# Value loads on a second DMA queue, and the last loads and products in another order: an adaLN attention and MLP block on one core

## The chip, the core and the metric

The kernel runs on one core of a Trainium2 chip. The core has engines that run side by side, each with its own instruction stream: TensorE (PE, matrix products, whose weight loads are listed as PEld), VectorE (DVE), ScalarE (ACT), GpSimd (POOL) and SyncE (SP, which only issues transfers). Transfers from main memory (HBM) to on-chip memory are carried by 16 DMA engines, which all queues share; a queue is where an engine puts the transfers it issues. The metric is the time on the device in microseconds, as the median over runs. A change of 0.2% is about the least that a measurement of this kernel can tell from none.

## The reference

Two tokens (B = 2, one position each, D = 512) go through one transformer block whose normalisations are shifted, scaled and gated by a condition `c`:

```
mod = (silu(c) @ w_mod).reshape(2, 6, 1, -1)            # sa, ca, ga, sb, cb, gb
h = layernorm(x) * (1 + ca) + sa
q = h @ wq                                              # 32 heads of 128
k, v = the last W = 4096 positions of k_cache, v_cache  # 8 key/value heads, each for 4 query heads
o = softmax(q k^T * 128**-0.5) v
x = x + ga * (o @ wo)
h = layernorm(x) * (1 + cb) + sb
x = x + gb * (silu(h @ w1) @ w2)                        # F = 1792
```

All is float32. There is little arithmetic for each byte: the weights and the two windows of the caches, 97.5 MB, are read once.

## The kernel before

**The ring.** All large loads go through one ring of eight slots (`slots`, 16 KB per partition each). `stream(n)` hands out the next n slots in turn, starting on a multiple of n where n is even. A load into a slot waits until all readers of what the slot held before are done. `load_pair(cache, s)` (L77) takes two slots for one step's keys or values (two key/value heads of one token, 4 MB), and `load_runs` (L88) takes as many as a stretch of rows of a weight needs. Both issue from SP, whose queue is worked off in order: a load whose slot is not free holds back all that stand behind it.

**The steps.** Attention runs in `STEPS` = 8 steps (L477). In step s, `keys(s, j)` (L356) has DVE transpose the keys in 32 x 32 blocks, in four parts; `scores(s, j)` (L366) multiplies each part with the queries on PE; `maxima` and `exponentials` (L382, L400) take the softmax on DVE and ACT; `turn(s)` (L415) brings the probabilities into the order that the value product needs (DVE, PE, then two ACT instructions that write `ptb`); `weighted(s)` (L445) is the value product on PE, 32 matmul instructions, which ends with an ACT copy to `ob`; `collect(s)` (L460) adds the result into `o_all`. The work is staggered: step s turns the probabilities of step s - 1 and forms their value product after its own scores. `place` (L312) lays out the queries; its first half runs before step 0, its second in step 2. The step before the last turns its own probabilities at its end.

**The loads around the steps.** `fetch(s)` (L349) issues the keys of step s and the values of step s - 1, so the order on SP is w_mod, x, wq, K0, K1, V0, K2, V1, K3, ... K7, V6, V7, and then wo in two loads (rows 0 to 23 of each partition's 32, then 24 to 31), w1 in two and w2 in four. In the ring this puts V7 into the slots of K6, the first wo load into those of V5 and the first of K7's, w1's first load into those of V6, the rest of w1 and the first w2 load into those of V7, and the later w2 loads into those of wo.

**The tail.** After the last step come the division by the row sums, the product with wo (`acc_o`, L579, and `ao`, L588), the residual and second normalisation, the product with w1 (`hid`, L627), silu, the product with w2 (`acc_yw`, L661, `acc_y`, `acc_l`) and the output. `busy(n)` (L562) puts n filler matmuls (two instructions each) on a scratch bank `junk` into PE's order at fixed places.

**Order.** A planner orders the instructions of each engine; an instruction marked with `inorder` (`tc.keep_in_program_order`) stays behind everything traced earlier on its engine. An unmarked one may move forward to where the planner takes its inputs as ready. The matmuls, transposes and copies of the steps are marked; the loads are not.

Of the kernel before, what the change touches and what calls it, by code (L numbers as in the profile page):

```python
# [23 lines left out]
def adaln_block(  # L24
# [19 lines left out]
    nc = tc.nc  # L44
# [19 lines left out]
    def bank(tag, name):  # L64
        return (psum1 if tag in "CO" else psum).tile([P, 512], F32, tag=tag, name=name)
# [4 lines left out]
    def stream(n=1):  # L70
        i = turn_of[0]
        if n % 2 == 0:
            i += -i % n
        turn_of[0] = i + n
        return slots[:, i % RING : i % RING + n, :].rearrange("p s e -> p (s e)")

    def load_pair(cache, s):  # L77


        i, b = divmod(s, B)  # L80
        t = stream(2)
        nc.sync.dma_start(
            t,
            cache[b, 2 * i : 2 * i + 2, SK - W :, :].rearrange("e (u n) d -> u e (n d)", u=P // 2),
        )
        return t

    def load_runs(w, per, lo, hi):  # L88

        e = w.shape[1]  # L90
        n = -(-(hi - lo) * e // 4096)
        t = stream(n)[:, : (hi - lo) * e].rearrange("p (q e) -> p q e", e=e)
        nc.sync.dma_start(t, w.rearrange("(p q) e -> p q e", q=per)[:, lo:hi, :])
        return t


# [2 lines left out]
    x_sp, c_sp = xc[:, 0, :], xc[:, 1, :]  # L99
    nc.vector.memset(xc, 0.0)  # L100
    wm = load_runs(w_mod, 4, 0, 4)
    rows8 = lambda t: t.rearrange("(ab r) m -> ab r m", r=16)[:, 0, :]
    for b in range(B):
        for lo in (0, 2):
# [3 lines left out]
            )  # L108
    nc.sync.dma_start(rows8(x_sp), x2.rearrange("b (g m) -> g b m", m=P))  # L109
    wqt = load_runs(wq, 4, 0, 4)  # L110


# [199 lines left out]
    def place(n):  # L312

        qT = once.tile([P, D], F32, tag="wide", name=f"qT{n}").rearrange("p (s j r) -> p s j r", s=4, r=32)
        inorder(nc.vector.transpose(qT.rearrange("p s j r -> p (s j r)"), q_ps[n]))  # L315
        for g in range(G):
            r = slice(32 * g, 32 * g + 32)
            eng = nc.gpsimd if g % 2 else nc.vector
            inorder(eng.tensor_copy(  # L319
                qg[n][r, :, :, :, g], qT[r, :, :, 0:32:16].rearrange("p s j b -> p s b j")  # L320
            ))
        rp = bank("C", f"qr{n}")[:, :P]
        inorder(nc.tensor.matmul(  # L323
            rp, rep4, qg[n].rearrange("p s b j g -> p (s b j g)"), start=True, stop=True
        ))
        for i in range(4):
            r = slice(32 * i, 32 * i + 32)
            cp = nc.scalar.copy if i % 2 else nc.vector.tensor_copy
            inorder(cp(
                qbd[n][r].rearrange("p s b j c -> p (s b j) c")[:, :, 4 * i : 4 * i + 4],  # L330
                rp[r, :].rearrange("p (m g) -> p m g", g=G),
            ))
# [12 lines left out]
    STEPS = B * HKV // 2  # L345
    kt, vt, wot, kT = {}, {}, [], {}
    s_ps, pr, o_ps, o_sb = {}, {}, {}, {}

    def fetch(s):  # L349

        if s < STEPS:
            kt[s] = load_pair(k_cache, s)
        if s > 0:
            vt[s - 1] = load_pair(v_cache, s - 1)

    def keys(s, j):  # L356


        kT[s, j] = ktp.tile([P, 64, 32], F32, tag="kT", name=f"kT{s}_{j}")
        for c in range(2):  # L360
            inorder(nc.vector.transpose(  # L361
                kT[s, j][:, 32 * c : 32 * c + 32, :],
                kt[s].rearrange("p (n j r) -> p j n r", j=4, r=32)[:, j, 32 * c : 32 * c + 32, :],
            ))

    def scores(s, j):  # L366

        if j == 0:
            s_ps[s] = bank("A", f"s{s}")
        i, b = divmod(s, B)  # L370
        for c in range(2):
            for e in range(2):
                r, h = 64 * e + 32 * c, 2 * i + e
                inorder(nc.tensor.matmul(  # L374
                    s_ps[s][r : r + 32, :],
                    qbd[h // 4][:, h % 4, b, j, :],
                    kT[s, j][:, 32 * c : 32 * c + 32, e:32:2],
                    start=(j == 0),
                    stop=(j == 3),
                ))  # L380

    def maxima(s):  # L382
        mx = work.tile([P, 1], F32, tag="mx", name=f"mx{s}")
        inorder(nc.vector.tensor_reduce(mx, s_ps[s], axis=AX.X, op=ALU.max))  # L384
        mT = bank("B", f"mT{s}")
        inorder(nc.tensor.matmul(mT[0:1, :P], mx, ident, start=True, stop=True))  # L386
        m = mrow[s % 2]
        mg = work.tile([1, 2, G], F32, tag="mg", name=f"mg{s}")
        inorder(nc.vector.tensor_reduce(
            mg,  # L390
            mT[0:1, :P].rearrange("o (e c i g) -> o e g c i", e=2, c=2, g=G)[:, :, :, :, 0:4],
            axis=AX.XY,
            op=ALU.max,
        ))
        inorder(nc.vector.tensor_copy(
            m.rearrange("o (e c i g) -> o e c i g", e=2, c=2, g=G)[:, :, :, 0:4, :],
            mg[:, :, None, None, :].to_broadcast([1, 2, 2, 4, G]),
        ))
# [16 lines left out]
    def turn(s):  # L415

        xp = once.tile([P, 16, 32], F32, tag="xp", name=f"xp{s}")
        inorder(nc.vector.transpose(xp, pr[s]))  # L418
        zp = once.tile([P, 4, 16, 16], F32, tag="zp", name=f"zp{s}")
        inorder(nc.vector.tensor_mul(  # L420
            zp,
            xp[:, None, :, 0:16].to_broadcast([P, 4, 16, 16]),
            quarter[:, :, None, None].to_broadcast([P, 4, 16, 16]),
        ))
        tp = bank("C", f"pT{s}")[:, : 2 * P]
        for i in range(4):
            inorder(nc.tensor.matmul(  # L427
                tp[32 * i : 32 * i + 32, :],
                mix.rearrange("p v e -> p (v e)"),
                zp.rearrange("p y t x -> p (y t) x")[:, :, 4 * i : 4 * i + 4],  # L430
                start=True,
                stop=True,
            ))
        for e in range(2):
            inorder(nc.scalar.activation(  # L435
                ptb[s % 2][:, :, e, :],
                tp.rearrange("p (w z) -> p w z", z=16),
                AF.Copy,
                scale=odd[:, e : e + 1],
            ))  # L440

    def weighted(s):


        o_ps[s] = bank("D", f"o{s}")  # L445
        for w in range(16):
            r = 32 * (w % 4)
            inorder(nc.tensor.matmul(  # L448
                o_ps[s][r : r + 32, :],
                ptb[s % 2][:, w].rearrange("p e z -> p (e z)"),  # L450
                vt[s].rearrange("p (c w m f d) -> p c f w m d", c=2, w=4, m=4, f=2)[
                    :, w // 8, w // 4 % 2, w % 4
                ],
                start=(w < 4),
                stop=(w >= 12),
            ))
        o_sb[s] = once.tile([P, 4 * DH], F32, tag="wide", name=f"ob{s}")
        inorder(nc.scalar.copy(o_sb[s], o_ps[s]))  # L458

    def collect(s):  # L460

        i, b = divmod(s, B)
        lo = 2 * HQ - 8 - (HQ * b + 2 * G * i)
        for m in range(4):
            r = 64 * (m % 2)
            inorder(nc.tensor.matmul(  # L466
                o_all[r : r + 64, :],
                selh[:, m, lo : lo + 2 * HQ],
                o_sb[s][:, m * DH : (m + 1) * DH],
                start=(s == 0 and m < 2),  # L470
                stop=(s == STEPS - 1 and m >= 2),
                skip_group_check=True,
            ))

    fetch(0)
    keys(0, 0)
    for s in range(STEPS + 1):  # L477
        if s < STEPS:
            fetch(s + 1)
            scores(s, 0)  # L480
        if s > 0 and s != STEPS - 1:
            turn(s - 1)
        if s > 1:
            collect(s - 2)
        if s == 2:
            place(1)
        if s < STEPS:
            for j in range(1, 4):
                keys(s, j)
                scores(s, j)  # L490
            maxima(s)
            exponentials(s)
        if s < STEPS - 2:
            keys(s + 1, 0)
        if s > 0:
            weighted(s - 1)
        if s == STEPS - 2:
            turn(s)
            keys(s + 1, 0)
# [2 lines left out]
    gaT, sbT, cbT = turned(ga, "gaT"), turned(sb, "sbT"), turned(cb1, "cbT")  # L502
    nc.gpsimd.tensor_copy(hT[:, :, 1:32:16], sbT[:, :, 0:32:16])
    ax = once.tile([P, P], F32, tag="ax", name="ax")
    for lo, hi in ((0, 24), (24, 32)):
        wt = load_runs(wo, 32, lo, hi)
        wot.extend(wt[:, q, :] for q in range(hi - lo))
    xT = turned(x_sp, "xT")
# [173 lines left out]
    for tt in range(11, T2):  # L682
        for h in range(2):
            for g in range(4):
                lo = g * P + h * H
# [46 lines left out]
```

## Time and profile before

| | |
|---|---|
| time, median of 3 runs | 235.59 us (235.44 to 235.62) |
| span of the profiled execution | 233.7 us |
| PE busy | 161.1 us (69%) |
| DVE busy | 115.6 us (49%) |
| ACT busy | 28.5 us (12%) |
| POOL busy | 10.5 us (4%) |
| read from HBM | 97.53 MB, 417 GB/s over the span |
| mean granted TensorE clock | 0.934 |

The span runs from the first to the last instruction of the program in one profiled execution; the times of the runs hold a little more at both ends. Lines of the profile name an instruction by its line in the kernel (L448), its engine, its operation and its tiles, written as output<-inputs. A suffix q on an engine (SPq, ACTq) means the engine's sequencer, which issues transfers. In a timeline, a number in brackets is the time for which the engine stood idle before the instruction, with what ended the wait. DMA share is the mean busy share of the 16 engines (a little over 1 where packets overlap).

### The profile page before, as it was taken

Reading aid. Unit: us, or ns where it says so; the run is one execution under the profiler, and the core shown is the slowest. Engines: PE = TensorE matmul, PEld = TensorE weight load, DVE = VectorE, ACT = ScalarE, POOL = GpSimd, SP = SyncE. Lnnn points to the kernel's source line nnn. Section 1 sums busy time; section 2 is a strip of 40 time slices with the busy share of each in tenths; the row PEclk is TensorE's granted clock in tenths of the full one; section 3 lists DMA queues with packets and bytes.
Section 4 is the critical chain, followed back from the end, with each engine's and each line's share of the span. In section 5 each row is a group of like instructions: output and inputs, shape, how many; then the busy total and the mean of one; then the engine's idle time right before and its main releaser. Section 6 shows DMA issues by size and latency. Waiting matters only on the chain.

```text
span 233.7 us, 2571 instructions
## 1 busy us (share of the span) xinstructions
PE 161.1 (69%) x1070; PEld 43.3 (19%) x1070; DVE 115.6 (49%) x179; ACT 28.5 (12%) x64; POOL 10.5 (4%) x35
## 2 busy tenths in 40 slices
PE   0004916859577839797598749759759779789684
PEld 0001401201111111211120201202112122324222
DVE  0007240278894758695197089259559540101232
ACT  2000210000311120120210201111020120102020
POOL 2004710000000000000000000000000000000000
PEclk9999985979999977999979999988997997999999
DMA  7998998999999999999999999999999999989991
GB/s 269 446 542 359 404 494 359 446 444 421 415 421 449 446 437 415 426 426 446 449 437 409 418 437 449 449 421 412 426 444 449 443 421 437 463 367 437 424 404 57
DMA packets 3794, 97.68 MB, mean 418 GB/s; under 512 B 432, under 2 KB 456, under 8 KB 968
## 3 DMA queue, kind: packets, MB, share of 16 engines
q1 hardware_dynamic: 3768, 97.53, 97.1%
q8 instruction: 8, 0.13, 0.2%
q14 instruction: 2, 0.02, 0.0%
q10 hardware_dynamic: 16, 0.00, 0.0%
HBM read 97.53 MB, written 0.00 MB: 417 GB/s over the span
## 4 chain that ended last, share of the span: by engine, by line
DMA 60%; issue 18%; DVE 14%; PE 6%; POOL 0%; SPq 0%; POOLq 0%; ACT 0%
DMA slots<-in_A_k_cache_dram 22%; DMA slots<-in_A_wq_dram 15%; DMA slots<-in_A_v_cache_dram 12%; DMA slots<-in_B_w_dram 12%; DVE kT L361 11%; PE o L448 2%; PE q L302 2%; DVE zp L420 1%; PE acc_yw L661 1%; DVE xp L418 1%; PE qr L323 0%; PE acc_y L671 0%; DVE qT L315 0%; POOL qg L319 0%; SPq L109 0%
## 5 line engine op out<-in xcount | busy, mean ns | idle before, releaser
L361 DVE STREAM_TRANSPOSE kT<-slots 128x1024 f32<-128x1024 f32 x64 | 73.7, 1212 | 23.7 <-DMA slots<-in_A_k_cache_dram 23.6
L374 PE MATMUL s<-kT,qbd 128*32 128x512 f32 x256 | 68.6, 693 | 19.1 <-DVE kT L361 18.0
L448 PE MATMUL o<-slots,ptb 128*32 128x512 f32 x256 | 30.8, 624 | 2.1 <-DMA slots<-in_A_v_cache_dram 2.1
L374 PEld LDWEIGHTS s<-kT,qbd 128*32 128x32 f32 x256 | 9.6, 113 | 68.4 <-DVE kT L361 63.4
L269 PE MATMUL m_a<-slots,scT 128*32 128x256 f32 x32 | 4.4, 506 | 20.5 <-DVE scT L261 20.5
L302 PE MATMUL q<-slots,hq_T 128*32 128x512 f32 x64 | 8.3, 680 | 7.0 <-DMA slots<-in_A_wq_dram 7.0
L448 PEld LDWEIGHTS o<-slots,ptb 128*32 128x32 f32 x256 | 8.1, 114 | 17.9 <-issue 17.8
L404 ACT COPY bias<-bp 128x1 f32<-128x1 f32 x8 | 1.3, 159 | 77.0 <-PE bp L402 77.0
L384 DVE TENSOR_REDUCE mx<-s 128x1 f32<-128x512 f32 x8 | 5.5, 691 | 9.6 <-PE s L374 9.6
L565 PE MATMUL junk<-quad,id 128*32 128x512 f32 x22 | 10.2, 595 | 0.0
L420 DVE TENSOR_TENSOR zp<-xp,quarter 128x1024 f32<-128x1024 f32 x8 | 9.8, 1225 | 0.2
L435 ACT ACTIVATE ptb<-pT,odd 128x256 f32<-128x256 f32 x16 | 6.7, 472 | 25.6 <-PE pT L427 25.6
L255 DVE STREAM_TRANSPOSE cT<-xc 128x128 f32<-128x128 f32 x1 | 0.4, 401 | 16.7 <-DMA xc<-in_c_dram 16.7
L427 PE MATMUL pT<-zp,mix 128*32 128x256 f32 x64 | 5.7, 428 | 3.6 <-DVE zp L420 3.5
L458 ACT COPY ob<-o 128x512 f32<-128x512 f32 x8 | 4.7, 585 | 26.1 <-PE o L448 26.1
L272 PE MATMUL m_sp<-slots,scT 128*32 128x512 f32 x32 | 7.4, 738 | 0.0
L386 PE MATMUL mT<-ident,mx 128*1 128x128 f32 x16 | 3.0, 270 | 6.3 <-DVE mx L384 6.3
L315 DVE STREAM_TRANSPOSE qT<-q 128x512 f32<-128x512 f32 x2 | 1.4, 717 | 11.7 <-PE q L302 10.2
L418 DVE STREAM_TRANSPOSE xp<-pr 128x512 f32<-128x512 f32 x8 | 5.5, 686 | 3.4 <-ACT pr L406 3.4
L579 PE MATMUL acc_o<-slots,oTn 128*32 128x512 f32 x56 | 6.2, 593 | 0.7 <-DMA slots<-in_A_wo_dram 0.7
L466 PE MATMUL o_all<-ob,selh 128*64 128x128 f32 x64 | 6.0, 316 | 0.8 <-ACT ob L458 0.8
L550 DVE COPY acc_o_sb<-acc_o 128x256 f32<-128x256 f32 x1 | 0.4, 425 | 12.4 <-ACT acc_o_sb L549 12.4
(140 smaller groups left out, 93.8 us busy)
## 6 DMA issues: line engine op xcount, KB each, us to landing
slots<-in_A_k_cache_dram SPq DMA_DIRECT2D x8, 4096.0 KB, 27.4
slots<-in_A_v_cache_dram SPq DMA_DIRECT2D x8, 4096.0 KB, 27.6
slots<-in_w_mod_dram SPq DMA_DIRECT2D x1, 6144.0 KB, 17.1
slots<-in_A_wo_dram SPq DMA_DIRECT2D x1, 6144.0 KB
slots<-in_B_w_dram SPq DMA_DIRECT2D x1, 2688.0 KB
slots<-in_A_wo_dram SPq DMA_DIRECT2D x1, 2048.0 KB, 29.5
slots<-in_B_w_dram SPq DMA_DIRECT2D x1, 2048.0 KB
slots<-in_B_w_dram SPq DMA_DIRECT2D x1, 896.0 KB
```

The source lines that it names most:

```text
L272: nc.tensor.matmul(m_sp[r, :], scT[:, k, :], cd[:, g], start=(k == 0), stop=(k == 3))
L302: nc.tensor.matmul(q_ps[n][32 * g : 32 * g + 32, :], hq_T[:, k, :], wv[:, n, g], start=(k == 0), stop=(k == 3),)
L361: inorder(nc.vector.transpose(kT[s, j][:, 32 * c : 32 * c + 32, :], kt[s].rearrange("p (n j r) -> p j n r", j=4, r=32)[:, j, 32 * c : 32 * ...
L374: inorder(nc.tensor.matmul(s_ps[s][r : r + 32, :], qbd[h // 4][:, h % 4, b, j, :], kT[s, j][:, 32 * c : 32 * c + 32, e:32:2], start=(j == ...
L418: inorder(nc.vector.transpose(xp, pr[s]))
L420: inorder(nc.vector.tensor_mul(zp, xp[:, None, :, 0:16].to_broadcast([P, 4, 16, 16]), quarter[:, :, None, None].to_broadcast([P, 4, 16, 16 ...
L427: inorder(nc.tensor.matmul(tp[32 * i : 32 * i + 32, :], mix.rearrange("p v e -> p (v e)"), zp.rearrange("p y t x -> p (y t) x")[:, :, 4 * ...
L435: inorder(nc.scalar.activation(ptb[s % 2][:, :, e, :], tp.rearrange("p (w z) -> p w z", z=16), AF.Copy, scale=odd[:, e : e + 1],))
L448: inorder(nc.tensor.matmul(o_ps[s][r : r + 32, :], ptb[s % 2][:, w].rearrange("p e z -> p (e z)"), vt[s].rearrange("p (c w m f d) -> p c f ...
L466: inorder(nc.tensor.matmul(o_all[r : r + 64, :], selh[:, m, lo : lo + 2 * HQ], o_sb[s][:, m * DH : (m + 1) * DH], start=(s == 0 and m < 2) ...
L565: inorder(nc.tensor.matmul(junk[0:32, :], id4, quad.rearrange("p m y -> p (m y)"), start=True, stop=True,))
L579: inorder(nc.tensor.matmul(acc[32 * g : 32 * g + 32, :], oTn[:, q, :], wot[q], start=(q < 4), stop=(q >= 24),))
```

## The change

Five edits. Value loads are issued from ScalarE's queue, key loads still from SP's. `fetch` takes one cache at a time: keys of step s + 1 at the head of step s as before, values of step s + 1 at its end, after the value product of step s - 1 (V0 is fetched at the head of step 0). In the last step the value product of step 6 is put ahead of the scores instead of behind them. wo is loaded in three pieces. The weight loads are marked to stay in program order on SP.

```
-        nc.sync.dma_start(
+        (nc.sync if cache is k_cache else nc.scalar).dma_start(
             t,
             cache[b, 2 * i : 2 * i + 2, SK - W :, :].rearrange("e (u n) d -> u e (n d)", u=P // 2),
         )
...
-        nc.sync.dma_start(t, w.rearrange("(p q) e -> p q e", q=per)[:, lo:hi, :])
+        tc.keep_in_program_order(
+            nc.sync.dma_start(t, w.rearrange("(p q) e -> p q e", q=per)[:, lo:hi, :])
+        )
...
-    def fetch(s):
+    def fetch(cache, s):
 
         if s < STEPS:
-            kt[s] = load_pair(k_cache, s)
-        if s > 0:
-            vt[s - 1] = load_pair(v_cache, s - 1)
+            (kt if cache is k_cache else vt)[s] = load_pair(cache, s)
...
-    fetch(0)
+    fetch(k_cache, 0)
     keys(0, 0)
     for s in range(STEPS + 1):
         if s < STEPS:
-            fetch(s + 1)
+            fetch(k_cache, s + 1)
+            if s == 0:
+                fetch(v_cache, 0)
+            if s == STEPS - 1:
+                weighted(s - 1)
             scores(s, 0)
...
         if s < STEPS - 2:
             keys(s + 1, 0)
-        if s > 0:
+        if 0 < s != STEPS - 1:
             weighted(s - 1)
+        fetch(v_cache, s + 1)
         if s == STEPS - 2:
             turn(s)
             keys(s + 1, 0)
...
-    for lo, hi in ((0, 24), (24, 32)):
+    for lo, hi in ((0, 16), (16, 24), (24, 32)):
```

Since slots are handed out in the order of these calls, the loads now take the ring's places in the order K0, K1, V0, V1, K2, V2, K3, V3, ... K7, V7. From K2 on keys take slots 0-1 and 4-5 by turns, from V1 on values take 6-7 and 2-3. wo's first load goes into K6's slots, its second and third into V6's; w1's first into K7's; the rest of w1 and w2's first into V7's; the later w2 loads into wo's.

## The prediction

> **What bounds the kernel now.** I read the page's DMA rows first, then DMA over two long windows, the chain of waits, and the instructions after the last value load.
>
> ```profile
> DMA  7998998999999999999999999999999999989991
> q1 hardware_dynamic: 3768, 97.53, 97.1%
> q10 hardware_dynamic: 16, 0.00, 0.0%
> ```
>
> The 16 DMA engines are busy to seven tenths or more in all 40 slices but the last, and mostly to nine. Nearly all bytes go through q1, SP's queue; q10 is ScalarE's, with the four tiny loads of c.
>
> ```profile
> 46.00:193.00 147.00, 110.33 (x639) 25.18 (x638) 99.47 (x115) 20.42 (x52) 0.49 (x2) 0.93 1.01 434
> 193.00:229.00 36.00, 30.82 (x244) 11.11 (x246) 5.17 (x23) 4.38 (x7) 0.00 (x0) 0.95 0.97 413
> ```
>
> The last two columns are DMA share and GB/s: 1.01 and 434 while keys and values stream, 0.97 in the last 36 us. There is no hole in the stream that an edit could fill. A 4096 KB load (4.194 MB) at 434 GB/s takes 9.66 us.
>
> ```profile
> 165.61 27.61 DMA slots<-in_A_v_cache_dram
> 193.21 0.14 issue
> 193.35 5.37 PE o L448 x32
> 198.74 27.57 DMA slots<-in_B_w_dram
> 226.30 0.14 issue
> 226.44 1.92 PE acc_yw L661 x16
> 230.78 0.27 DVE yo L702 x2
> ```
>
> In the chain of waits (start, us, what) the last value load, V7, is issued at 165.61, as soon as K6 is transposed, because V7 goes into K6's slots. It lands at 193.21; its product runs to 198.74; the weights that take its slots end the stream, and the w2 products start at 226.44. So the end is set by the DMA stream. But a second path, of compute, starts at V7's landing. Its rows in the timeline (idle before in brackets):
>
> ```profile
> 201.91 5.34 PE L565 MATMUL junk<-quad,id 128*32 128x512 f32 x12
> 202.01 0.27 DVE L542 COPY oTn<-oq 128x64 f32<-128x64 f32 x1 [1.26 <-PE oq L539]
> 207.91 6.22 PE L579 MATMUL acc_o<-slots,oTn 128*32 128x512 f32 x56 [0.66 <-DMA slots<-in_A_wo_dram]
> 219.46 1.71 PE L627 MATMUL hid<-slots,hT_b 128*32 128x448 f32 x16 [1.30 <-DMA slots<-in_B_w_dram]
> 226.44 1.92 PE L661 MATMUL acc_yw<-slots,uT 128*32 128x512 f32 x16 [0.76 <-DMA slots<-in_B_w_dram]
> ```
>
> PE waits for a DMA only three times from V7's product to the end: 0.66 us for wo, 1.30 for w1, 0.76 for w2. Sum 2.72 us. That is all the slack of this path: the filler matmuls on `junk` (L565) run whether they are needed or not. If V7's product starts x us later, the end comes x - 2.72 us later.
>
> **The change, part by part.** *Two queues.* No byte is added, and 434 GB/s at a share of 1.01 leaves nothing to gain by issuing from a second queue. What changes is the order of landing. How two queues share the engines, the trace shows where c's loads meet the w_mod load; in the DMA view of 7.8 to 9.6 us:
>
> ```profile
> DMA packets 18, 0.79 MB, mean 437 GB/s; under 512 B 2, under 2 KB 2, under 8 KB 2
> q1 hardware_dynamic: 16, 0.79, 100.8%
> q10 hardware_dynamic: 2, 0.00, 0.1%
> ```
>
> In the time of one w_mod packet per engine (16 packets of q1), q10 gets two packets, though four loads of it have long been waiting. I read this as turns: one packet of each queue. Keys and values have packets of one size, so while both queues hold work each load takes twice 9.66 us.
>
> *Which slots.* The ring holds four loads. After the change keys alternate between slots 0-1 and 4-5 (from K2 on) and values between 2-3 and 6-7 (from V1 on). V7 now takes V5's slots and waits for V5's product; the first wo load takes K6's slots and waits only for K6's transposes. These stood so:
>
> ```profile
> 172.44 0.58 ACT L458 COPY ob<-o 128x512 f32<-128x512 f32 x1 [2.63 <-PE o L448]
> 182.01 1.41 SPq L93 DMA_DIRECT2D slots<-in_A_wo_dram  x2
> ```
>
> V5's product ended at 172.44, 6.8 us after K6's slots came free (165.61); wo was issued at 182.01, after V7. So wo(0,16), 4.194 MB, moves from behind V7 to ahead of it or beside it. One load of 9.66 us is put in V7's way.
>
> *When V7 lands, term by term.*
>
> ```profile
> 43.97 0.54 SPq L82 DMA_DIRECT2D slots<-in_A_v_cache_dram  x1
> 47.01 0.26 ACT L329 COPY qbd<-qr 32x128 f32<-32x128 f32 x1 [0.35 <-DVE qbd L329]
> 48.23 1.25 DVE L361 STREAM_TRANSPOSE kT<-slots 128x1024 f32<-128x1024 f32 x1 [1.25 <-DMA slots<-in_A_k_cache_dram]
> ```
>
> K0 is in at 48.2; from there to 193.2 fifteen loads land, 9.67 us each, which agrees with the window. V0's slots are free at 43.97; on ScalarE its issue may fall behind the two qbd copies (end 47.27), so the value queue starts between 44.5 and 48.2. Eight value loads in turns take 8 x 2 x 9.67 = 154.7 us: V7 at 199.2 to 202.9, if its queue never runs dry. Whether it does, rows of two steps tell:
>
> ```profile
> 77.15 2.37 DVE L361 STREAM_TRANSPOSE kT<-slots 128x1024 f32<-128x1024 f32 x2 [2.71 <-DMA slots<-in_A_k_cache_dram]
> 99.71 0.54 SPq L82 DMA_DIRECT2D slots<-in_A_v_cache_dram  x1
> 115.80 2.37 DVE L361 STREAM_TRANSPOSE kT<-slots 128x1024 f32<-128x1024 f32 x2 [5.52 <-DMA slots<-in_A_k_cache_dram]
> 126.84 0.53 SPq L82 DMA_DIRECT2D slots<-in_A_k_cache_dram  x1
> 133.66 0.53 SPq L82 DMA_DIRECT2D slots<-in_A_v_cache_dram  x1
> ```
>
> In an ordinary step a key load's slots come free 11.0 us after it landed (115.80 to 126.84), and the product of the value load before it is done after 17.9 us (133.66). Key loads then land 19.3 us apart, so the key queue never runs dry, and the value queue only just not. In step 2, which also places the second half of q, the product is done 22.6 us after K2 (77.15 to 99.71). K2 lands at 84 to 87 (K1 and K2 at half rate behind 48.2, less what K1 gets alone), so V3 is issued at 106.5 to 109.5, while V2 is through at 58 us after V0's start, 102.5 to 106.2. The value queue stands dry for 0 to 7 us, the longer the earlier V0 began. That makes V7 202.9 to 206.2 on either start; once wo(0,16) is through, V7 meets packets of half the size and gains under 1 us. I take **204.0**, 10.7 us later than the 193.35 of its product's start; ends 199.2 and 206.2.
>
> The Trainium skill, "DMA: Bandwidth & Descriptors", Queues, rings and completion order, says an engine drains a whole packet, typically 9 to 17 descriptors, from one row before it switches. By that a load's share per engine would go in one turn, loads would land whole and alternate, and V7 would come after sixteen loads behind K0, 48.2 + 16 x 9.67 = 202.9, a result 1.1 us better than mine; the two-to-sixteen row above speaks for finer turns. The same page's Rules for kernel authors hold that spreading loads over issuing engines gains no bandwidth, only issue time; the rows of 434 GB/s agree.
>
> *V6's product ahead of the last scores.* PE now stands at V6 while K7 is being transposed; behind it in PE's order wait scores(7) and all that follows.
>
> ```profile
> 179.24 4.97 PE L374 MATMUL s<-kT,qbd 128*32 128x512 f32 x24
> 184.25 0.69 DVE L384 TENSOR_REDUCE mx<-s 128x1 f32<-128x512 f32 x1 [1.19 <-PE s L374]
> 190.42 0.84 ACT L435 ACTIVATE ptb<-pT,odd 128x256 f32<-128x256 f32 x2
> ```
>
> V6 lands some 18 us ahead of V7, at 186; its product takes 5.4 us (193.35 row), the scores of a step with keys ready 3.6 to 5.4, and from the last score to ptb 7.0 us (184.25 to 191.26): ptb at 202 to 203.8. V7 at 204.0 covers it, barely; without that cover up to 1 us. It costs 0 here and is inside the range.
>
> *Issues on ScalarE* cost 0.49 us each (row below), eight in all. Behind each stands the ptb pair of the next step, which waits for PE anyway:
>
> ```profile
> L105 ACTq DMA_DIRECT2D xc<-in_c_dram x4: 485/488/1076, 1.2 to 3.3; - x4
> ACT ptb L435 <- PE pT L427: 25.6, 6, 6.4
> ```
>
> The wait the issue adds is on the product that the ob copy just ahead waits for, so it is 0; without the cover it is 0.5 us a step. *wo in three loads* is one issue more on SP (0.7 us, half of the 182.01 row), while loads of many us are queued: 0. The w2 loads behind V7's product are issued 10 us later, but by then wo(16,32) and w1, 6.95 MB or 16 us, are queued, so w2 is in before 230, ahead of its products.
>
> **Sum.** V7's product +10.7, slack -2.7: +8.0 us. The profiled span of 233.7 becomes 241.7; the median of the runs stands 1.9 us above that span, so 235.6 becomes **243.6**. With V7's ends: 199.2 gives +3.1 (238.7), 206.2 gives +10.1 (245.7).
>
> **Rivals.** *A: not slower.* The key queue runs dry, and values get the engines alone for that time; each us brings V7 1 us earlier. For it: K3 now waits for V0's product, in a step where K2 is due at the same time. Against: from K4 on, keys are released 8 us ahead of need. It decides from 204.0 - 196.1 = 7.9 us of dryness: then the 2.72 us of slack cover V7, the stream ends as now, and the time is 235.6, or up to 0.8 less if w2 lands sooner. *B: worse still.* The value queue is dry in most steps, since 17.9 us and an issue stand against 19.3; 1 us in each of five steps and 7 in step 2 put V7 at 208 to 211 and the time at 248 to 250. For it: the margin is that thin; against: if the value queue lags, its load lands later than the key load beside it and the margin grows. *C: whole loads in order of issue*, so that the second queue changes nothing in sharing. V7 still comes after wo(0,16), which is issued first: 202.9, +6.8, 242.4, inside the forecast's range.
>
> **Chances.** Forecast with C: 0.74. A: 0.13, of it 0.07 faster by over 0.2% and 0.06 within it (0.2%, 0.5 us, is what a measurement here can tell from no change). B: 0.13. Slower is 0.87. The likeliest case's own range is 238.7 to 245.7; for 8 in 10 I take 238.0 to 247.5, which leaves out A and the far part of B.
>
> **What would show it.** In the changed trace q10 carries 33.6 MB. K1 should land at 63 to 68, clearly more than 9.67 us behind K0, since it shares the engines with V0. wo(0,16) is issued before V7. The L448 product of V7 starts near 204, and the waits for wo, w1 and w2 on PE (0.66, 1.30, 0.76) are gone: acc_yw then waits for DVE's uT alone, and DMA is no longer busy in the slice before the last. The forecast is wrong if V7's product starts before 197, or if the DMA share between 60 and 190 us falls under 0.97.

## The result, and the profile after

| | before | after |
|---|---|---|
| time, median of 6 runs each | 235.57 us (235.35 to 235.62) | 246.62 us (245.17 to 248.31) |
| ratio, 95% interval | 1 | 1.0473 (1.0451 to 1.0495) |
| span of the profiled execution | 233.7 us | 245.1 us (its own time 246.8) |
| DMA, HBM read over the span | 97.53 MB, 417 GB/s | 97.53 MB, 398 GB/s |

The change makes the kernel 4.7% slower. Executions more than 1.5% above the fastest of their kernel count in the medians and ranges below but not in the ratios (two of six with the second queue alone, one of four with the late product). On the page of the changed kernel, the DMA digits of the 40 slices and the two queues stand so:

```profile
DMA  7999999999999999999999999999999999999500
q1 hardware_dynamic: 2760, 63.97, 61.3%
q10 hardware_dynamic: 1168, 33.56, 31.8%
```

The stream is hardly slower while it runs (430 GB/s below, against 434 before over the same stretch), but it stops early: the last two slices are empty, where before it ran into the last. The values, 33.56 MB, now go through q10. Three stretches after, each with its length, the busy time of PE, PEld, DVE, ACT and POOL, and last the granted clock, DMA share and GB/s:

```profile
46.00:193.00 147.00, 101.14 (x564) 22.81 (x564) 96.01 (x107) 18.25 (x46) 0.49 (x2) 0.87 1.00 430
...
206.00:229.00 23.00, 21.48 (x173) 7.72 (x166) 1.30 (x4) 2.60 (x5) 0.00 (x0) 0.88 1.00 423
...
229.00:245.00 16.00, 12.10 (x146) 4.62 (x140) 5.31 (x25) 2.62 (x5) 0.00 (x0) 1.00 0.06 23
```

The last 16 us are compute with hardly a byte moving. Which compute, the timeline shows (the bracket is the idle time of the engine before, with what ended it):

```profile
172.34 0.34 SPq L94 DMA_DIRECT2D slots<-in_A_wo_dram  x1
...
179.18 0.54 ACTq L82 DMA_DIRECT2D slots<-in_A_v_cache_dram  x1
...
190.24 5.70 PE L448 MATMUL o<-slots,ptb 128*32 128x512 f32 x32 [10.70 <-DMA slots<-in_A_v_cache_dram]
...
200.42 0.69 DVE L384 TENSOR_REDUCE mx<-s 128x1 f32<-128x512 f32 x1 [10.65 <-PE s L374]
...
206.65 0.84 ACT L435 ACTIVATE ptb<-pT,odd 128x256 f32<-128x256 f32 x2 [3.21 <-PE pT L427]
...
207.57 5.57 PE L448 MATMUL o<-slots,ptb 128*32 128x512 f32 x32
...
221.10 6.14 PE L584 MATMUL acc_o<-slots,oTn 128*32 128x512 f32 x52
...
237.69 1.92 PE L666 MATMUL acc_yw<-slots,uT 128*32 128x512 f32 x16
```

wo's first load is issued at 172.34, 6.8 us ahead of V7 (179.18). V7's product starts at 207.57, where it started at 193.35. From there to the end PE waits for no transfer: the brackets with 0.66, 1.30 and 0.76 us are gone.

The product of step 7 does not wait for V7 itself. The row ahead of it is `ptb`, which ends at 207.49, and the chain of waits goes from there back to V6, not V7:

```profile
159.59 30.52 DMA slots<-in_A_v_cache_dram
...
190.24 5.70 PE o L448 x32
195.94 0.92 PE s L374 x8
...
200.42 0.70 DVE mx L384
...
207.64 5.55 PE o L448 x32
```

V6 is issued at 159.59 and lands at 190.1; its product, put ahead of the last scores, holds PE to 195.94; scores, softmax and `ptb` follow. V7 was in only a little before. The DMA view of 179 to 180 us lists its issue with the time from there to its landing:

```profile
slots<-in_A_v_cache_dram ACTq DMA_DIRECT2D x1, 4096.0 KB, 27.8
```

That is 179.18 + 27.8 = 207.0. Two paths end within some 0.5 us of each other: V7's landing, 13.8 us later than before (193.2), and `ptb`, 16 us later (191.3). The mean granted clock is lower too (0.889 against 0.934), but it cannot account for the 11 us behind the product of step 7: that part of the kernel takes as long as before, as the sum on the slack below shows.

### The profile page after: what moved, and what is told of

Same layout as the page of the kernel before. It is cut to its first block, busy times and chain, and to the rows that moved or that the text cites. A ratio compares the mean times of both kernels' runs of the same rounds, so it can differ in the third digit from the quotient of the medians.

```text
span 245.1 us, 2573 instructions
## 1 busy us (share of the span) xinstructions
PE 160.8 (66%) x1070; PEld 43.4 (18%) x1070; DVE 115.8 (47%) x179; ACT 28.7 (12%) x64; POOL 10.5 (4%) x35
## 3 DMA queue, kind: packets, MB, share of 16 engines
q10 hardware_dynamic: 1168, 33.56, 31.8%
HBM read 97.53 MB, written 0.00 MB: 398 GB/s over the span
## 4 chain that ended last, share of the span: by engine, by line
DMA 52%; PE 32%; DVE 11%; issue 1%; ACTq 1%; ACT 1%; DVEq 0%
DMA slots<-in_A_k_cache_dram 34%; DMA slots<-in_A_v_cache_dram 12%; PE s L374 8%; PE o L448 8%; DMA xc<-in_c_dram 6%; DVE kT L361 6%; PE junk L570 4%; PE acc_o L584 2%; PE m_sp L274 2%; DVE zp L420 1%; PE hid L632 1%; PE o_all L466 1%; PE m_a L271 1%; DVE mx L384 1%; ACTq L107 1%
## 5 line engine op out<-in xcount | busy, mean ns | idle before, releaser
L374 PE MATMUL s<-kT,qbd 128*32 128x512 f32 x256 | 66.1, 711 | 22.3 <-DVE kT L361 21.3
L448 PE MATMUL o<-slots,ptb 128*32 128x512 f32 x256 | 33.1, 663 | 10.7 <-DMA slots<-in_A_v_cache_dram 10.7
L304 PE MATMUL q<-slots,hq_T 128*32 128x512 f32 x64 | 8.8, 710 | 8.1 <-DMA slots<-in_A_wq_dram 8.1
L427 PE MATMUL pT<-zp,mix 128*32 128x256 f32 x64 | 7.0, 521 | 2.9 <-DVE zp L420 2.8
L257 DVE STREAM_TRANSPOSE cT<-xc 128x128 f32<-128x128 f32 x1 | 0.4, 402 | 16.9 <-DMA xc<-in_c_dram 16.9
L584 PE MATMUL acc_o<-slots,oTn 128*32 128x512 f32 x56 | 7.0, 593 | 0.0
L274 PE MATMUL m_sp<-slots,scT 128*32 128x512 f32 x32 | 6.6, 712 | 0.0
```

Of the source, the lines that this page charges most:

```text
L274: nc.tensor.matmul(m_sp[r, :], scT[:, k, :], cd[:, g], start=(k == 0), stop=(k == 3))
L304: nc.tensor.matmul(q_ps[n][32 * g : 32 * g + 32, :], hq_T[:, k, :], wv[:, n, g], start=(k == 0), stop=(k == 3),)
L374: inorder(nc.tensor.matmul(s_ps[s][r : r + 32, :], qbd[h // 4][:, h % 4, b, j, :], kT[s, j][:, 32 * c : 32 * c + 32, e:32:2], start=(j == ...
L427: inorder(nc.tensor.matmul(tp[32 * i : 32 * i + 32, :], mix.rearrange("p v e -> p (v e)"), zp.rearrange("p y t x -> p (y t) x")[:, :, 4 * ...
L448: inorder(nc.tensor.matmul(o_ps[s][r : r + 32, :], ptb[s % 2][:, w].rearrange("p e z -> p (e z)"), vt[s].rearrange("p (c w m f d) -> p c f ...
L584: inorder(nc.tensor.matmul(acc[32 * g : 32 * g + 32, :], oTn[:, q, :], wot[q], start=(q < 4), stop=(q >= 24),))
```

## The experiments

The theory: the product of step 7 is late on two paths. V7 lands late, because its slots come free late and wo's first load is served beside it. And V6's landing plus some 17 us (early product, last scores, last softmax) is as late. From that product on, PE needs 37.6 us to the end whatever the stream does. The rivals: the second queue costs as such; or V7's landing is all there is; or the early product is. Each time below is a median; the kernel before took 235.5 to 235.6 beside each.

### The change on one queue

```
-        (nc.sync if cache is k_cache else nc.scalar).dma_start(
+        nc.sync.dma_start(
```

> The changed kernel with the value loads back on SP's queue; slots, order of calls, early product of step 6 and wo in three loads stay. Theory (the new slots put V3 behind the product of step 1, and in one queue K4 and all later loads stand behind that wait): the stream gets holes of some us, first before V3 near 105 to 109, V7 lands at 196 to 200 and the time is 239 to 243, below 246.6 since wo now stands behind V7. Rival (the second queue as such is the cost, by slower transfers or by stalls on ScalarE): back to 235.6 to 236.5.

249.9 us (249.6 to 250.3), ratio 1.0607 (1.0586 to 1.0628): slower than the change itself. Two stretches of its DMA (the last columns are share and GB/s) and later rows of its timeline:

```profile
104.00:112.00 8.00, 6.68 (x64) 2.27 (x60) 6.59 (x9) 1.89 (x5) 0.00 (x0) 1.00 0.20 61
112.00:120.00 8.00, 6.86 (x30) 0.95 (x26) 6.34 (x7) 0.48 (x2) 0.00 (x0) 1.00 0.95 403
```

```profile
110.30 0.54 SPq L82 DMA_DIRECT2D slots<-in_A_v_cache_dram  x1
110.93 0.56 SPq L82 DMA_DIRECT2D slots<-in_A_k_cache_dram  x1
...
193.89 9.13 DVE L361 STREAM_TRANSPOSE kT<-slots 128x1024 f32<-128x1024 f32 x8 [3.21 <-DMA slots<-in_A_k_cache_dram]
...
211.37 4.61 PE L448 MATMUL o<-slots,ptb 128*32 128x512 f32 x32
```

The hole is where the theory put it: the stream falls to a share of 0.20 until V3 is issued at 110.30, and K4 goes out right behind it. The time is some 7 us above the range, because the end comes by a path that neither side named: K7, behind such a wait as well, lands only at 193.9, and its transposes, scores and softmax take 17.4 us to the end of `ptb`. V7, issued at 191.30, is in 13.6 us later, at 204.9; the product of step 7 waits for `ptb` until 211.37. The rival falls: without the second queue the new order of slots is worse, not cured. Given those slots, the second queue fills the hole.

### The second queue alone

The kernel before, with this one edit:

```
-        nc.sync.dma_start(
+        (nc.sync if cache is k_cache else nc.scalar).dma_start(
             t,
             cache[b, 2 * i : 2 * i + 2, SK - W :, :].rearrange(...),
```

> The kernel before with one edit: value loads go through ScalarE's queue; slots, order of calls, products and wo as before. Theory (what costs is the wo load beside V7 and the order of the last products, not the queue): V7 sits in K6's slots and wo waits for K7's transposes, so the value queue has the engines alone for about the 11 us between; V7's product starts at 193 to 196 and the time is 235.6 to 237.5. Rival (the second queue as such costs): 243 or more.

238.0 us (236.6 to 241.8), 1.0075 (1.0043 to 1.0107). By the medians the queue costs 2.5 us of the 11, a little over the range expected; by the ratio 1.8 us, inside it. Both are far from 243. The start of V7's product was missed by 4 us:

```profile
173.79 0.16 ACT L404 COPY bias<-bp 128x1 f32<-128x1 f32 x1 [8.36 <-PE bp L402]
173.87 0.54 ACTq L82 DMA_DIRECT2D slots<-in_A_v_cache_dram  x1
...
187.85 1.41 SPq L93 DMA_DIRECT2D slots<-in_A_wo_dram  x2
...
199.80 5.34 PE L448 MATMUL o<-slots,ptb 128*32 128x512 f32 x32 [2.73 <-DMA slots<-in_A_v_cache_dram]
```

V7 is issued at 173.87, not at 165.61: K6 came later (its transposes end at 170.53), and the planner had set the issue behind the bias copy on ScalarE. That is not what makes V7 late: V6, ahead of it on the same queue, lands only at 184.6. From 178.2 to 191.2 us the value queue does have the engines alone (5.67 MB). But wo, issued at 187.85, comes in just before V7 is through. The DMA view of 191.4 to 200 us has

```profile
q1 hardware_dynamic: 72, 3.54, 95.3%
q10 hardware_dynamic: 22, 0.20, 5.4%
```

The 0.20 MB are the last 6 of V7's 128 data packets. Served between wo's, they delay its landing to 199.7 (173.87 + 25.8 from its issue). The product starts at 199.80, 6.5 us later than before; less 2.7 of slack that is 3.7, and the span grew by 3.2 (233.7 to 236.9). The late V7 accounts for it, and here too by wo beside it; no other cost of the queue is needed.

### V7 ahead of wo

```
-        (nc.sync if cache is k_cache else nc.scalar).dma_start(
+        (nc.sync if cache is k_cache or s == 7 else nc.scalar).dma_start(
```

> The changed kernel with V7 alone issued from SP, ahead of wo. Theory of two paths of nearly equal length (V7's landing, and V6's landing + 17.3 us through the product of step 6, the last scores and the last softmax): V7 lands near 196, ten us sooner, but its product still waits for ptb, at V6's landing (188 to 190) + 17.3 = 205.5 to 207.5; the time falls by 0 to 2 us, 244.5 to 246.6. Rival (V7's landing alone sets the end, as the prediction had it): product at 196, time 236 to 238.

240.1 us (238.8 to 242.1), 1.0198 (1.0129 to 1.0267): between the two. In the timeline:

```profile
180.28 0.54 SPq L82 DMA_DIRECT2D slots<-in_A_v_cache_dram  x1
...
183.95 5.34 PE L448 MATMUL o<-slots,ptb 128*32 128x512 f32 x32 [3.30 <-DMA slots<-in_A_v_cache_dram]
```

and in the chain of waits:

```profile
183.95 5.34 PE o L448 x32
...
193.69 0.70 DVE mx L384
...
200.81 4.39 PE o L448 x32
```

The number was missed because V6 landed at 183.9 and not at 188 to 190: with wo held behind V7, SP's queue ran dry near 180 (from 178.7 to 181.5 q1 starts no data packet) and V6 had the engines alone. The mechanism held: V6 + 16.9 us = 200.8 is where the product of step 7 starts, and it waits for `ptb`, with no DMA wait of its own.

### The second half of the queries a step later

```
-        if s == 2:
+        if s == 3:
             place(1)
```

> The changed kernel with the second half of the queries laid out in step 3 instead of step 2. Theory (the value queue stands dry before V3 because step 2 takes 22.6 us from K2's landing to the product of step 1; that dryness is passed on to V6 and V7): V3 is issued 3 us sooner, V6 and V7 land 2 to 3 us sooner, and the time falls by 2 to 3 us, to 243.5 to 244.6. Rival (the dryness is made up later, or moves to V4): no change, 246 to 247.

246.0 us (245.1 to 248.1), 1.0427 (1.0391 to 1.0463): no change that its spread could show. V3 and V4 were issued at

```profile
105.04 0.54 ACTq L82 DMA_DIRECT2D slots<-in_A_v_cache_dram  x1
...
130.14 0.54 ACTq L82 DMA_DIRECT2D slots<-in_A_v_cache_dram  x1
...
191.89 5.51 PE L448 MATMUL o<-slots,ptb 128*32 128x512 f32 x32 [12.30 <-DMA slots<-in_A_v_cache_dram]
```

instead of 109.11 and 124.32. V3 came 4 us sooner and V4 6 us later, and V6 still landed near 192. The rival was right: the dry time moved by one step and was not removed.

### The early product alone

The kernel before, with this:

```
             fetch(s + 1)
+            if s == STEPS - 1:
+                weighted(s - 1)
             scores(s, 0)
...
-        if s > 0:
+        if 0 < s != STEPS - 1:
             weighted(s - 1)
```

> The kernel before with one edit: the product of step 6 ahead of the last scores. Theory: V6 lands near 184, its product takes 5.4 us, the scores 4 to 5, and ptb follows 7 us after, at 200.4 to 201.5; the product of step 7 starts there and not at 193.35; less the slack of 2.7 us that is 4.3 to 5.4 us, a time of 239.9 to 241. Rival (V7's landing at 193 sets the end, and the early product is covered by it, as the prediction costed it): 235.6.

239.8 us (239.3 to 239.9), 1.0173 (1.0156 to 1.0190), 0.1 us under the range.

```profile
184.10 6.49 PE L448 MATMUL o<-slots,ptb 128*32 128x512 f32 x32 [10.92 <-DMA slots<-in_A_v_cache_dram]
...
194.98 0.69 DVE L384 TENSOR_REDUCE mx<-s 128x1 f32<-128x512 f32 x1 [11.53 <-PE s L374]
...
201.20 0.84 ACT L435 ACTIVATE ptb<-pT,odd 128x256 f32<-128x256 f32 x2 [3.19 <-PE pT L427]
...
202.14 4.31 PE L448 MATMUL o<-slots,ptb 128*32 128x512 f32 x32
```

With V7 in time, moving one product ahead of the last scores costs 4.2 us by itself: PE stands 10.9 us waiting for V6 while the scores it could do are queued behind.

### The late product in the changed kernel

The same edit undone in the changed kernel:

```
-            if s == STEPS - 1:
-                weighted(s - 1)
             scores(s, 0)
...
-        if 0 < s != STEPS - 1:
+        if s > 0:
             weighted(s - 1)
```

> The changed kernel with the product of step 6 behind the last scores again, as before. Theory of two paths (V7 is in at 206; the early product holds ptb back to 207.5): the last softmax is done well before V7, the product of step 7 starts when V7 lands, 206 to 206.6, and the time falls by 1 to 1.6 us, to 245.0 to 245.6. Rival (the early product alone is what costs the 11 us): ptb near 198, and the time falls to 237 to 239.

245.8 us (244.8 to 249.0), 1.0422 (1.0381 to 1.0463). Against the change's own spread (245.2 to 248.3) a gain of 0.8 us is not shown. The profiled execution is the longest of its four (249.0), so only what each instruction waited for is read:

```profile
197.06 0.84 ACT L435 ACTIVATE ptb<-pT,odd 128x256 f32<-128x256 f32 x2
...
207.09 6.58 PE L448 MATMUL o<-slots,ptb 128*32 128x512 f32 x32 [9.22 <-DMA slots<-in_A_v_cache_dram]
```

`ptb` is done at 197.9, and the product now waits 9.2 us for V7. The path through V6 is gone and the time is hardly less: V7 was just as late.

### Both edits

V7 on SP ahead of wo, and the product of step 6 behind the last scores.

> Both edits: V7 alone on SP ahead of wo, and the product of step 6 behind the last scores. Theory of two paths: V7 lands at 192 to 196 and ptb no longer waits for V6; from K7 at 180.2 nine us of transposes and seven from the last score give ptb at 197, the product of step 7 at 197.3, 4.0 us later than in the kernel before, and 236.8 (236.3 to 237.5); so the two edits together give some 10 us, where the first alone gave 6.5 and the second 1 to 1.6. Rival (the paths are not what sets the end; the rest is the cost of two queues): 239 to 240, as with the first edit alone.

236.8 us (235.8 to 239.3, 10 runs), 1.0063 (1.0033 to 1.0093).

```profile
196.94 0.84 ACT L435 ACTIVATE ptb<-pT,odd 128x256 f32<-128x256 f32 x2
...
197.84 3.64 PE L448 MATMUL o<-slots,ptb 128*32 128x512 f32 x32
...
227.34 1.92 PE L664 MATMUL acc_yw<-slots,uT 128*32 128x512 f32 x16 [0.85 <-DMA slots<-in_B_w_dram]
```

The product starts at 197.84, and the w2 products wait for a transfer again (0.85 us): the stream sets the end as it did before. The two edits alone gave 6.5 and 0.8 us, together 9.8. That is how two paths of almost one length behave. This kernel keeps the new slots, the second queue for the other seven value loads and wo in three pieces: together they cost no more than the 1.2 us that are left.

### The fillers, in both kernels

```
-    busy(6)
     for q in range(28):
```

In the changed kernel:

> The changed kernel without the six filler matmuls ahead of acc_o. Theory (from V7's product on, the end is set by PE's path, not by the stream): acc_o starts 4.8 to 5.2 us sooner, and the time falls by 3 to 5.2 us, to 241.4 to 243.6; less than 5.2 only if w1, w2 or a lower granted clock takes some back. Rival (the stream still sets the end): no change, 246 to 247.

In the kernel before:

> The kernel before without the six filler matmuls ahead of acc_o. Theory (there the stream sets the end, and PE's path has slack): PE waits some 5 us longer for wo, and the time stays at 235.4 to 236.0, where the same edit took 6.2 us off the changed kernel. Rival (the filler is on the path in both): 230 to 231.

Changed kernel: 240.4 us (239.7 to 242.8), 6.2 less than with them, one us below the range expected. Kernel before: 235.7 us, ratio 1.0005 (0.9992 to 1.0019), no change; its timeline there reads

```profile
208.28 8.49 PE L578 MATMUL acc_o<-slots,oTn 128*32 128x512 f32 x56 [7.60 <-DMA slots<-in_A_wo_dram]
```

The same six matmuls cost nothing where PE waits for wo anyway (7.6 us without them, 0.66 with them), and about their full time where it doesn't (5.2 us by their rows after; the 6.2 measured is not told apart from that by runs that scatter by 3 us). This separates the two limits directly: before, the stream; after, PE's path behind V7's product.

### w2's first load in halves

The kernel before, with w2 loaded so:

```
-    for lo, hi in ((0, WIDE), (WIDE, 11), (11, 13), (13, T2)):
+    for lo, hi in ((0, 4), (4, WIDE), (WIDE, 11), (11, 13), (13, T2)):
```

> The kernel before with w2's first load (8 of 14 rows of each partition) in two halves. Theory: acc_yw waits 0.76 us for 2 MB of which its first half needs only 1; with the halves apart it starts when uT is ready, 225.7, and its second half is done 0.2 to 1 us sooner than now: 234.6 to 235.4. Rival (the end hangs on the last bytes of w2, not on these): 235.5, no change.

235.7 us, 1.0010 (1.0001 to 1.0019): nothing gained. In its timeline `acc_yw` starts without a DMA wait, but the next ones have it:

```profile
226.24 1.93 PE L661 MATMUL acc_yw<-slots,uT 128*32 128x512 f32 x16
...
228.43 0.86 PE L671 MATMUL acc_y<-slots,uT 128*32 128x128 f32 x24 [0.26 <-DMA slots<-in_B_w_dram]
...
229.75 0.89 PE L686 MATMUL acc_l<-slots,uT 128*32 128x64 f32 x48 [0.16 <-DMA slots<-in_B_w_dram]
```

The wait has only moved on to the products behind, as the rival has it, and no version tried here beats the kernel before.

## Why the prediction was right, and where its sizes were off

**What bounds each kernel.** Right. The stream bound the kernel before, and PE's path from V7's product bounds the changed one; the filler runs show it by one edit with 6.2 us in the one and none in the other.

**The slack of 2.72 us.** Right. From the start of V7's product the changed kernel needs 245.1 - 207.57 = 37.5 us; the kernel before, less its three waits, 233.7 - 193.35 - 2.72 = 37.6. With the measured start the sum is 207.57 - 193.35 - 2.72 = 11.5 us, and the span grew by 11.4.

**Turns.** Right. From 90 to 100 us, with both queues full, q10 started 68 packets and q1 64:

```profile
q10 hardware_dynamic: 68, 2.23, 51.6%
q1 hardware_dynamic: 64, 2.10, 48.5%
```

K1 was taken up at 66.49 (DVE's timeline), inside the 63 to 68 foretold:

```profile
66.49 2.37 DVE L361 STREAM_TRANSPOSE kT<-slots 128x1024 f32<-128x1024 f32 x2 [6.13 <-DMA slots<-in_A_k_cache_dram]
```

This does not fit whole loads taken by turns, which is how the row of the Trainium skill ("DMA: Bandwidth & Descriptors", Queues, rings and completion order) was read for loads of this size: in 10 us about one load passes, and it was half of each queue.

**V7's landing, forecast 204.0.** The mechanism was right and the term was too small: this step failed in size. wo's load did go out ahead of V7 and was served beside it, and the value queue did stand dry before V3. But the terms as worked out gave 202.9 to 206.2, and V7 landed at 207.0, above them all. The dry time was put at 0 to 7 us and came to over 8. In the DMA view of 105 to 113.2 us of the changed kernel q10 is absent, and q1 alone has

```profile
q1 hardware_dynamic: 96, 3.05, 92.2%
```

V3 was issued at 109.11, inside the 106.5 to 109.5 foretold; its first packet starts at 113.2, some 4.1 us later. The sum has no term for that, and why it takes so long was not traced; with the change on one queue, and the DMA engines idle, it was 1.3 us (110.30 to 111.6). A part of the loss came back: the keys had run ahead meanwhile, K5 had to wait for K3's transposes (issue at 117.48), and from 116 to 122 us q10 moved 2.13 MB against 0.46. How much of V7's lateness is dry time and how much wo beside it was not separated. The run with the queries a step later adds that the dry time isn't a matter of step 2 alone.

**The early product, costed at 0.** Here the cover did not hold. The terms behind V6 were right: 5.7 us for the product, 4.5 for scores, 7.1 to the end of `ptb`, 17.3 in all. But V6 was put at 186 and landed at 190.1, late for the same reason as V7, so `ptb` came at 207.5 and not by 203.8. On top of V7 it costs some 0.5 us by the trace, which the runs cannot tell from none; alone, in the kernel before, it costs 4.2. Its cover was V7's own lateness, which is no cover for a version that cures V7: with V7 ahead of wo 3.3 us were still lost to it (240.1 against 236.8).

**What hides the issues on ScalarE, and the third wo load.** No row of the changed kernel speaks against 0. The run with the second queue alone shows a case that the prediction did not have: an issue placed behind a bias copy went out 3.3 us after its slots came free (170.53 to 173.87). It cost nothing there, because V6 still held the queue.

**The rivals.** A (the key queue runs dry) did happen in the changed kernel, where its argument put it: K3 had to wait for V0's product and was issued only at 84.42, and in the DMA view of 84.3 to 88.3 us the queues have

```profile
q10 hardware_dynamic: 64, 1.57, 92.0%
q1 hardware_dynamic: 2, 0.00, 0.0%
```

These 4 us are half of the 7.9 that A needed, and they brought V2 in sooner, but V3 had to wait for its slots all the same. In the run with V7 on SP the key queue ran dry near 180 as well, and there it brought V6 in by 184. B (dry in most steps) lies at 248 to 250; the result stands between it and the forecast, by the longer dry time of one step: q10 has no second pause of this kind. C differs from the forecast by the turns above.

**The range.** 246.6 lies within 238.0 to 247.5, though above the likeliest case's own 238.7 to 245.7, by the two sizes named above. The margin of the range had to cover a term that the sum did not have; that it was enough is in part luck, since pauses of the key queue, which the forecast left out, gave some time back.

## What to carry to other kernels

A second queue gave no bandwidth to a stream that was already full (430 GB/s against 434); what it changes is which load lands first, so ask of each load on a compute path what is now served beside it, and whose slots it must wait for. When a kernel is bound by its stream, add up the transfer waits on the compute path behind the last input: that sum, here 2.7 us, is all that input may be late. And an instruction moved forward in an in-order engine brings its wait with it: a product that waits for a load should not stand ahead of work whose inputs are already there, even where it seems to be covered by something equally late.

## What the runs showed that was not expected

The kernels with both queues full scatter more than those with one: 245.2 to 248.3 us for the change, 236.6 to 238.7 for four of six with the second queue alone and 240.9 and 241.8 for the others, 238.8 to 242.1 with V7 on SP, against 235.2 to 236.5 in 21 runs of the kernel before, 249.6 to 250.3 for the change on one queue and 239.3 to 239.9 for the early product alone. The two with fillers or scores changed on two queues scatter alike (239.7 to 242.8, 244.8 to 249.0). What differs between two runs of one program there was not traced, and the cause is open.
